# Attention and two mixtures of experts in one kernel: three branch programs for each expert of the second mixture, three up tiles of the next expert issued between the join and the next branch, and attention pieces in another order

## The chip, the cores and the metric

The kernel runs on one core of one Trainium2 chip. The metric is the device time of one execution in microseconds (us); the time shown is the median of 3 runs. The trace is one further execution, taken by the hardware profiler. The engines are named as in the trace: PE is the matrix engine (PEld its weight loads, PEq or PEldq its sequencers), DVE the vector engine, ACT the scalar engine, POOL GpSimd, SP the engine that issues most of the transfers.

## The reference, cut to what matters

Three stages stand one behind the other.

```python
# 1. chunked linear recurrence: 4 batches x 8 heads x 768 steps, head 32, state 16
M = (Cc @ Bc.T) * exp(cum_i - cum_j) * causal
y = M @ xc + (Cc @ state) * exp(cum)
state = exp(sum(la)) * state + (Bc * exp(cum_last - cum)).T @ xc
# 2. dense mixture: 3072 tokens of width 256, 4 experts, hidden width 1024
out += p[:, e:e+1] * (relu(x @ w1[e]) @ w2[e])
# 3. routed mixture: 8 experts, one per token, at most 768 tokens each
expert = argmax(x @ w_gate); gate = softmax(x @ w_gate)[expert]
out[i] = gate[i] * (relu(x[i] @ w1[expert]) @ w2[expert])
```

With the inputs used here the eight experts of stage 3 get 836, 313, 184, 362, 215, 164, 196 and 802 tokens; what is over 768 is dropped.

## The kernel before

All matmuls of the mixtures are done as three products of a high and a low part (`w1h`, `w1l`, `xh`, `xl` and so on), so each tile of 128 hidden units needs six matmuls for the up product (two halves of the width 256, three products) and three per block of 128 tokens for the down product.

**Stages 1 and 2 are interleaved.** The dense mixture walks over seven batches of 128-token steps (BLOCKS: 2, 3, 4, 4, 4, 4, 3 steps). For each batch it runs four experts of eight hidden tiles; after each tile it calls `tick(b)`, a slot, so that there are two slots for each tile. A slot issues what a table has put at this slot (`at_slot`: weight splits, loads), then some of the side pieces: the attention of the following batch's steps, one group after the other, spread evenly over the slots by the formula in `tick`, which begins at slot `wait` (11 for batch 0, else 0). One attention step is the list of groups in `USUAL`: pack B and C into high and low parts (`high`, `low`; the low parts are written by DVE at L198, those of C into the one buffer `cbd`), a running product over the step (`prefix`, a scan by DVE, L206), the decay matrices (`decay`, scans by DVE, L174), the scores on PE (L221, which read `bp` and `cbd`), masks (L239), products (L251), the split of the result, and the next step's loads. Every engine works off its own instructions in the order in which the program issues them. The scheduler adds the semaphores.

**Stage 3 walks over the experts.** For each expert e from 1 on, all engines read its token count (`values_load`, on PE a TENSOR_LOAD at L1028) and branch at L1032: over 256 tokens the wide program (`first_block` with 384 token columns, then `second_block`, which branches at L757: over 384 tokens a second block of 384 is done), else the narrow program (256 columns). Both end in a join, from which the next expert's count and branch follow. Expert 0 is done outside of this with 384 columns and its own second block. So with these counts the path is: e0 with a second block, e1 wide without one, e2 narrow, e3 wide without one, e4, e5 and e6 narrow, e7 wide with a second block. `ahead_of(e + 1)` marks the place of an instruction by which PE's sequencer is told in advance that a branch of the next expert lies ahead and where it likely goes; it is the first thing in each block.

`expert_block` runs the eight up tiles (L719 to L721, the relu to `gh` on ACT at L724, the low part `gl` on DVE at L725) and, behind them by LAG = 2 tiles, the down products (L736 to L738). `extra` are the next expert's row loads, transposes (`turn`, L689) and weight splits, issued between tiles.

Of the kernel before, what the change touches and what calls it, by code (L numbers as in the profile page):

```python
# [29 lines left out]
BIG = 1 << 20  # L30
SLOTS = 384
NARROW = 256
BLOCKS = [2, 3, 4, 4, 4, 4, 3]
MOST = max(BLOCKS)
NMAX = MOST * P
# [30 lines left out]
def attention_moe_moe_kernel(ctx: ExitStack, tc: tile.TileContext, aps: dict, cap: int):  # L66
# [88 lines left out]
    def attention_pieces(s, xH, xL, col):  # L155
# [151 lines left out]
            split=[split_high, split_low], state=[state_up], keep=[keep])  # L307

    USUAL = [g.split() for g in (
        "high0", "low0 high1", "", "low1 high2", "", "prefix0 low2 load2 load1", "", "decay0", "scores0", "mask0",  # L310
        "decay1 load0", "scores1 state_in0", "", "mask1", "", "products0", "split0", "split1 state0")]
    FIRST = [g.split() for g in (
        "prefix0 load2", "decay0", "", "scores0 decay1", "load0 load1", "state_in0", "mask0", "mask1", "", "products0", "split0",
# [383 lines left out]
            nc.scalar.copy(xh[:, d], t[d])  # L697
            nc.vector.tensor_tensor(xl[:, d], t[d], xh[:, d].bitcast(F32), ALU.subtract)

    def expert_block(e, k, n, extra):  # L700
        w1h, w1l, w2h, w2l = W[2, e]
        xh, xl = xs[e, k]
        g = gi[e, k]
        hs = {}
        y = []
        at_ = 0

        def go():
            nonlocal at_
            at_ += 1  # L710
            for p in extra.get(at_, []):
                p()

        for f in range(NF + LAG):
            if f < NF:
                ph = ps.tile([P, n], F32, tag="ph", name=f"qh{e}_{k}_{f}")
                for d in range(KD):
                    c = slice(FF * d + P * f, FF * d + P * f + P)
                    nc.tensor.matmul(ph, lhsT=w1h[:, c], rhs=xh[:, d, :n], start=d == 0, stop=False)  # L719
                    nc.tensor.matmul(ph, lhsT=w1h[:, c], rhs=xl[:, d, :n], start=False, stop=False)  # L720
                    nc.tensor.matmul(ph, lhsT=w1l[:, c], rhs=xh[:, d, :n], start=False, stop=d == KD - 1)  # L721
                hh = hp_.tile([P, n], F32R, tag="hh", name=f"gh{e}_{k}_{f}")
                hl = hp_.tile([P, n], F32R, tag="hl", name=f"gl{e}_{k}_{f}")
                nc.scalar.activation(hh, ph, AF.Relu)  # L724
                nc.vector.scalar_tensor_tensor(hl, ph, 0.0, hh.bitcast(F32), ALU.max, ALU.subtract)  # L725
                hs[f] = (hh, hl)
                go()
            js = [f - LAG] if LAG <= f < NF else list(range(NF - LAG, NF)) if f == NF else []
            for st in range(n // P):
                if js and js[0] == 0:  # L730
                    y.append(ps.tile([P, DM], F32, tag="acc", name=f"yy{e}_{k}_{st}", bufs=3))
                q = slice(P * st, P * st + P)
                for j in js:
                    hh, hl = hs[j]
                    c = slice(DM * j, DM * j + DM)
                    nc.tensor.matmul(y[st], lhsT=hh[:, q], rhs=w2h[:, c], start=j == 0, stop=False)  # L736
                    nc.tensor.matmul(y[st], lhsT=hh[:, q], rhs=w2l[:, c], start=False, stop=False)  # L737
                    nc.tensor.matmul(y[st], lhsT=hl[:, q], rhs=w2h[:, c], start=False, stop=j == NF - 1)  # L738
            if js:
                go()  # L740
        for st in range(n // P):
            o = gp.tile([P, ROW], F32, tag="row", name=f"yo{e}_{k}_{st}", bufs=MOST)[:, :DM]
            nc.scalar.activation(o, y[st], AF.Copy, scale=g[:, st, 0:1])  # L743
            i = nc.gpsimd.indirect_dma_start(  # L744
                out=out[:, :],
                out_offset=bass.IndirectOffsetOnAxis(ap=g.bitcast(I32)[:, st, 1:2], axis=0),
                in_=o[:, :], in_offset=None, bounds_check=TOK - 1, oob_is_err=False)
            disjoint("out", i)
# [4 lines left out]
            tc.mark_branch_hint_location(f"wide{e}", "LikelyTaken", engines=[mybir.EngineType.PE])  # L753

    def second_block(e, tokens):
        if nblk > 1:
            with tc.If(tokens > SLOTS, label=f"more{e}"):  # L757
                ahead_of(e + 1)
                expert_block(e, 1, SLOTS, {})
                for k in range(2, nblk):  # L760
                    with tc.If(tokens > SLOTS * k):
                        load_rows(e, k)
                        turn(e, k)
                        turned(e, k)
                        expert_block(e, k, SLOTS, {})


    new_xT(0)
# [119 lines left out]
    for b, i, e, c in (  # L888
# [23 lines left out]
    def tick(b):  # L912
        nonlocal slot, done
        nslot = 2 * sum(v[0] == b for v in seq)
        for fn in wq.get((b, slot), []):
            fn()
        if b == 1 and fills and slot % 3 == 2:
            fills.pop(0)()
        if b == 1 and slot == nslot - 1:
            while fills:  # L920
                fills.pop(0)()
        if urgent:
            urgent.pop(0)()
        wait = 11 if b == 0 else 0
        while done < len(side) and done < math.ceil((slot + 1 - wait) * len(side) / (nslot - 6 - wait)):
            side[done]()
            done += 1
        slot += 1
# [58 lines left out]
    for e, k in ahead:  # L987
        place(e, k)

    def first_block(e, n):  # L990
        extra = {}

        def add(i, fn):
            extra.setdefault(i, []).append(fn)

        add(0, lambda: ahead_of(e + 1))
        if n == SLOTS and nblk > 1:
            add(1, lambda: load_rows(e, 1))
            add(6, lambda: turn(e, 1))
            add(8, lambda: turned(e, 1))  # L1000
        if e + 1 < E2:
            add(1, lambda: load_rows(e + 1, 0))
            add(10, lambda: turn(e + 1, 0))
            add(12, lambda: turned(e + 1, 0))
        for c in range(4 if e + 2 < E2 else 0):
            m, i = (4, 6, 8, 10)[c], 4 * (e + 2) + c
            add(m, lambda w=order[i], lo=(nc.vector if c in (1, 2) else nc.gpsimd): split_w(2, *w, lo))
            if i + 5 < len(order):
                add(m + 3, lambda w=order[i + 5]: load_w(2, *w))
        for fn in extra.pop(0):  # L1010
            fn()
        expert_block(e, 0, n, extra)

    known = nc.values_load(cnt[0][0:1, 0:1], min_val=0, max_val=TOK)
    with tc.If(known > SLOTS - 1) as full:
# [2 lines left out]
    with full.Else():  # L1018
# [5 lines left out]
        turn(0, 0)  # L1024
        turned(0, 0)
        expert_block(0, 0, SLOTS, {4: [finish_ahead]})
    for e in range(E2):
        tokens = nc.values_load(cnt[1][0:1, e:e + 1], min_val=0, max_val=TOK)  # L1028
        if e == 0:
            second_block(e, tokens)  # L1030
            continue
        with tc.If(tokens > NARROW, label=f"wide{e}") as wide:  # L1032
            first_block(e, SLOTS)
            second_block(e, tokens)
        with wide.Else():
            first_block(e, NARROW)


def prepare(inputs):
# [51 lines left out]
```

## Time and profile before

| | |
|---|---|
| median of 3 runs | 809.57 us (809.2 to 809.78) |
| profiled execution | 811.7 us |
| its span in the trace | 809.9 us |
| PE busy | 774.8 us (96%) |
| DVE busy | 435.3 us (54%) |
| ACT busy | 283.4 us (35%) |
| POOL busy | 198.0 us (24%) |

The profiled execution is 2.1 us longer than the median of the runs, and 1.8 us of its time lie outside of the span that the trace shows. Busy shares are means over stages: stages 1 and 2 run to about 620 us, stage 3 behind them to about 805 us.

### The profile page before, as it was taken

To read this page: it belongs to the slowest core of one execution; us is meant where nothing else is said; L and a number is where in the kernel's file an instruction comes from. 1 tells how busy PE (TensorE), PEld (TensorE's weight loads), DVE (VectorE), ACT (ScalarE), POOL (GpSimd) and SP (SyncE) were. 2 spreads that over 40 slices of the span, in tenths; PEclk is the share of its full clock that TensorE was granted. 3 is DMA by queue.
4 is the path that set the end of the run, shared out by engine and by line. 5 is a ranking of instruction groups with operands and counts; after the bars stand their busy time and mean duration, and the time that the engine had idled before them with its cause. 6 is when DMAs were issued, how large, how long until landed. Compare 5 with 4: busy or idle time off the path is not lost. (4 is left out here: it accounts for less than half of the span.)

```text
span 809.9 us, 12519 instructions
## 1 busy us (share of the span) xinstructions
PE 774.8 (96%) x4752; PEld 688.7 (85%) x4752; DVE 435.3 (54%) x839; ACT 283.4 (35%) x550; POOL 198.0 (24%) x223
## 2 busy tenths in 40 slices
PE   9999989999999999999999999999999996968997
PEld 7889988977888778878788888889999896968997
DVE  5786777566664566655656546542534323524431
ACT  1443433323333232233322332322454333536432
POOL 1010202222110131211212202111665322525321
PEclk9999999999999999999999999999999998979999
DMA  8662677522210232202322013040353304544100
GB/s 256 219 188 78 209 206 212 171 82 102 81 61 18 82 108 82 82 0 82 105 82 82 28 55 108 14 140 11 114 159 104 115 21 143 158 141 131 32 23 28
DMA packets 50987, 83.26 MB, mean 103 GB/s; under 512 B 5136, under 2 KB 35809, under 8 KB 50908
## 3 DMA queue, kind: packets, MB, share of 16 engines
q1 hardware_dynamic: 47140, 75.30, 29.5%
q0 software_dynamic: 2400, 6.11, 2.1%
q10 hardware_dynamic: 1368, 0.81, 0.5%
q8 instruction: 49, 0.80, 0.4%
q14 instruction: 30, 0.25, 0.1%
HBM read 66.36 MB, written 16.31 MB: 102 GB/s over the span
## 5 line engine op out<-in xcount | busy, mean ns | idle before, releaser
L496 DVE SCALAR_TENSOR_TENSOR hl<-ph,hh 128x512 fp32r<-128x512 f32 (+2 forms) x216 | 133.5, 618 | 230.6 <-ACT hh L495 223.8
L495 ACT ACTIVATE hh<-ph 128x512 fp32r<-128x512 f32 (+2 forms) x216 | 117.2, 543 | 349.6 <-PE ph L492 342.0
L490 PE MATMUL ph<-xh,w1h 128*128 128x512 f32 (+2 forms) x432 | 160.4, 371 | 1.2 <-DVE hl L496 1.2
L519 PE MATMUL acc<-hh,w2h 128*128 128x512 f32 (+2 forms) x432 | 158.4, 367 | 1.1 <-DVE x L535 1.0
L491 PE MATMUL ph<-xl,w1h 128*128 128x512 f32 (+2 forms) x432 | 156.5, 362 | 0.0
L492 PE MATMUL ph<-xh,w1l 128*128 128x512 f32 (+2 forms) x432 | 156.3, 362 | 0.0
L520 PE MATMUL acc<-hl,w2h 128*128 128x512 f32 (+2 forms) x432 | 156.3, 362 | 0.0
L521 PE MATMUL acc<-hh,w2l 128*128 128x512 f32 (+2 forms) x432 | 156.1, 361 | 0.0
L725 DVE SCALAR_TENSOR_TENSOR gl<-qh,gh 128x384 fp32r<-128x384 f32 (+1 forms) x80 | 40.2, 503 | 106.0 <-ACT gh L724 97.6
L519 PEld LDWEIGHTS acc<-hh,w2h 128*128 128x128 f32 x432 | 81.2, 188 | 13.7 <-issue 2.0
L543 POOL TENSOR_TENSOR x<-x,cmb 128x512 f32<-128x512 f32 (+2 forms) x40 | 49.0, 1245 | 176.8 <-DVE cmb L540 176.8
L490 PEld LDWEIGHTS ph<-xh,w1h 128*128 128x128 f32 x432 | 81.3, 188 | 12.2 <-issue 1.7
L492 PEld LDWEIGHTS ph<-xh,w1l 128*128 128x128 f32 x432 | 81.2, 188 | 10.5
L521 PEld LDWEIGHTS acc<-hh,w2l 128*128 128x128 f32 x432 | 81.3, 188 | 10.4
L520 PEld LDWEIGHTS acc<-hl,w2h 128*128 128x128 f32 x432 | 81.3, 188 | 9.3
L491 PEld LDWEIGHTS ph<-xl,w1h 128*128 128x128 f32 x432 | 81.3, 188 | 8.7
L724 ACT ACTIVATE gh<-qh 128x384 fp32r<-128x384 f32 (+1 forms) x80 | 35.9, 448 | 92.5 <-PE qh L721 87.2
L174 DVE TENSOR_TENSOR_SCAN lt<-abc,id 128x512 f32<-128x512 f32 x44 | 59.6, 1354 | 0.1
L738 PE MATMUL yy<-w2h,gl 128*128 128x256 f32 x208 | 59.1, 284 | 0.0
L737 PE MATMUL yy<-w2l,gh 128*128 128x256 f32 x208 | 59.1, 284 | 0.0
L736 PE MATMUL yy<-w2h,gh 128*128 128x256 f32 x208 | 59.1, 284 | 0.0
L719 PE MATMUL qh<-sxh,w1h 128*128 128x384 f32 (+1 forms) x128 | 43.5, 340 | 16.3 <-issue 14.8
(156 smaller groups left out, 1075.2 us busy)
## 6 DMA issues: line engine op xcount, KB each, us to landing
stg<-in_w SPq DMA_DIRECT2D x34, 512.0 KB, 4.2
abc<-a_zero SPq DMA_DIRECT2D x21, 512.0 KB, 5.6
bcr<-in_bc SPq DMA_DIRECT2D x19, 512.0 KB, 3.9
disp<-zrow SPq DMA_DIRECT2D x12, 516.0 KB, 6.1
nat<-in_nat SPq DMA_DIRECT2D x24, 256.0 KB, 6.5
rw<-disp SPq DMA_DIRECT2D x12, 387.0 KB, 4.3
pb<-pT SPq DMA_DIRECT2D x16, 256.0 KB, 4.1
out<-zrow SPq DMA_DIRECT2D x6, 512.0 KB, 4.8
```

Source lines behind the costliest of these rows:

```text
L174: nc.vector.tensor_tensor_scan(t["lt"][:, sl, :].rearrange("p h i -> p (h i)"), a_bc[:, sl, :].rearrange("p h i -> p (h i)"), id4.rearrang ...
L490: nc.tensor.matmul(ph[:, :n], lhsT=wh[:, c], rhs=xh[:, k, :n], start=k == 0, stop=False)
L491: nc.tensor.matmul(ph[:, :n], lhsT=wh[:, c], rhs=xl[:, k, :n], start=False, stop=False)
L492: nc.tensor.matmul(ph[:, :n], lhsT=wl[:, c], rhs=xh[:, k, :n], start=False, stop=k == KD - 1)
L495: nc.scalar.activation(hh[:, :n], ph[:, :n], AF.Relu)
L496: nc.vector.scalar_tensor_tensor(hl[:, :n], ph[:, :n], 0.0, hh[:, :n].bitcast(F32), ALU.max, ALU.subtract)
L519: nc.tensor.matmul(a[:, :n], lhsT=wh[:, c], rhs=hh[:, :n], start=f == 0, stop=False)
L520: nc.tensor.matmul(a[:, :n], lhsT=wh[:, c], rhs=hl[:, :n], start=False, stop=False)
L521: nc.tensor.matmul(a[:, :n], lhsT=wl[:, c], rhs=hh[:, :n], start=False, stop=f == NF - 1)
L736: nc.tensor.matmul(y[st], lhsT=hh[:, q], rhs=w2h[:, c], start=j == 0, stop=False)
L737: nc.tensor.matmul(y[st], lhsT=hh[:, q], rhs=w2l[:, c], start=False, stop=False)
L738: nc.tensor.matmul(y[st], lhsT=hl[:, q], rhs=w2h[:, c], start=False, stop=j == NF - 1)
```

## The change

In words:

- **Three programs.** For e of 1 to 7 the branch on the second block is moved to the front: the wide program is chosen first (L1056), and inside it the choice between "384 and a second block" and "384 alone" (L1058). Three whole programs stand in the code for each expert, and `first_block` no longer tests for a second block in its middle. The row load and transposes for the second block are issued in that one program alone. `preferred_fallthrough_block` says which of the two programs stands right behind the branch.
- **A head behind each join.** `head(e + 1)` runs for every path between the join of expert e and the branch of expert e + 1: it marks the hint again and issues the first three up tiles (HEAD = 3) of the next expert for its first 256 columns. The block that follows only adds columns 256 to 383 of these tiles where it is wide (128-column matmuls), and begins at the fourth tile where it is narrow.
- **A fixed ring.** The tiles `hh` and `hl` come from three fixed pairs instead of the pool, since the head's tiles are read by other blocks. Six one-column memsets on POOL set them up.
- **Attention.** `USUAL` has `low1 high2` and `low2` two groups sooner, ahead of `prefix0`; `decay0` one group sooner; the loads in two groups. `wait` is 4 instead of 0 for batches 1 and on. Four weight splits of batch 1 go to the slots 7, 19, 31, 42 instead of 8, 16, 24, 32.

```diff
+HEAD = 3
     USUAL = [g.split() for g in (
-        "high0", "low0 high1", "", "low1 high2", "", "prefix0 low2 load2 load1", "", "decay0", "scores0", "mask0",
+        "high0", "low0 high1", "low1 high2", "low2 load1", "prefix0 load2", "", "decay0", "", "scores0", "mask0",
...
+    def make_ring():
+        for i in range(3):
+            ring.append([hp_.tile([P, NMAX], F32R, tag=t, name=f"ring_{t}{i}") for t in ("hh", "hl")])
+            for v in ring[-1]:
+                nc.gpsimd.memset(v.bitcast(F32)[:, 0:1], 0.0)
+    def up_part(e, k, f, a, b):
+        w1h, w1l = W[2, e][:2]
         xh, xl = xs[e, k]
+        ph = ps.tile([P, b - a], F32, tag="ph", name=f"qh{e}_{k}_{f}")
+        for d in range(KD):
+            c = slice(FF * d + P * f, FF * d + P * f + P)
+            nc.tensor.matmul(ph, lhsT=w1h[:, c], rhs=xh[:, d, a:b], start=d == 0, stop=False)
...
+        hh, hl = [v[:, a:b] for v in ring[f % len(ring)]]
+        nc.scalar.activation(hh, ph, AF.Relu)
+        nc.vector.scalar_tensor_tensor(hl, ph, 0.0, hh.bitcast(F32), ALU.max, ALU.subtract)
+    def head(e):
+        if e < E2:
+            ahead_of(e)
+            for f in range(HEAD):
+                up_part(e, 0, f, 0, NARROW)
+    def expert_block(e, k, n, extra, have=0):
...
             if f < NF:
-                ph = ps.tile([P, n], F32, tag="ph", name=f"qh{e}_{k}_{f}")
...
+                a = NARROW if f < have else 0
+                if a < n:
+                    up_part(e, k, f, a, n)
                 go()
...
-            (1, 8, 0, 2), (1, 16, 0, 3), (1, 24, 0, 0), (1, 32, 0, 1)):
+            (1, 7, 0, 2), (1, 19, 0, 3), (1, 31, 0, 0), (1, 42, 0, 1)):
...
-        wait = 11 if b == 0 else 0
+        wait = 11 if b == 0 else 4
...
+    make_ring()
...
-        if n == SLOTS and nblk > 1:
+        if two:
             add(1, lambda: load_rows(e, 1))
...
-        expert_block(e, 0, n, extra)
+        expert_block(e, 0, n, extra, HEAD)
...
-        with tc.If(tokens > NARROW, label=f"wide{e}") as wide:
-            first_block(e, SLOTS)
-            second_block(e, tokens)
-        with wide.Else():
-            first_block(e, NARROW)
+            with tc.If(tokens > NARROW, label=f"wide{e}", preferred_fallthrough_block=True) as wide:
+                if nblk > 1:
+                    with tc.If(tokens > SLOTS, preferred_fallthrough_block=False) as more:
+                        first_block(e, SLOTS, two=True)
+                        second_block(e, tokens)
+                    with more.Else():
+                        first_block(e, SLOTS)
...
+            with wide.Else():
+                first_block(e, NARROW)
+        head(e + 1)
```

The two places that matter most are shown by the instructions on an engine. The first is PE at the join of expert 1 and the branch of expert 2, before: the last down product of e1 (`yy_0_1`), the jump to the join, the count, the branch, and the first tile (`qh_0_0`) of the first program in the code.

```order
L738 MATMUL yy_0_1_7338<-w2h_1_5754,gl_0_7_7442 128x256
L1032 UNCONDITIONAL_BRANCH
L1028 TENSOR_LOAD cnt_97
L1032 COMPARE_AND_BRANCH
L1087 BRANCH_PREFETCH_HINT
L719 MATMUL qh_0_0_7490<-sxh_5732,w1h_2_5934 128x384
```

After, the branch stands behind the head: the rows below are the last six of its 18 matmuls of 256 columns (tiles `qh_0_0`, `qh_0_1`, `qh_0_2`), then the count, the two branches and the first 128-column matmul of the wide program.

```order
L717 MATMUL qh_0_2_7599<-sxh_5732,w1h_2_5934 128x256
L718 MATMUL qh_0_2_7599<-sxl_5733,w1h_2_5934 128x256
L719 MATMUL qh_0_2_7599<-sxh_5732,w1l_2_5935 128x256
L717 MATMUL qh_0_2_7599<-sxh_5732,w1h_2_5934 128x256
L718 MATMUL qh_0_2_7599<-sxl_5733,w1h_2_5934 128x256
L719 MATMUL qh_0_2_7599<-sxh_5732,w1l_2_5935 128x256
L1050 TENSOR_LOAD cnt_97
L1056 COMPARE_AND_BRANCH
L1058 COMPARE_AND_BRANCH
L1118 BRANCH_PREFETCH_HINT
L717 MATMUL qh_0_0_7991<-sxh_5732,w1h_2_5934 128x128
```

What moved: between the jump out of the last block and the branch now stand a hint and 18 matmuls that do not depend on the count; the wide program behind the branch begins with six 128-column matmuls per tile for three tiles.

The second is DVE in the attention step whose scores PE runs at 265 us. `cbd` is the low part of C, `pre` the prefix scan, `lt` a decay scan, `hl` the low part of a relu and `cmb` a combine of the dense mixture. Before:

```order
L198 SCALAR_TENSOR_TENSOR cbd<-bcr_2566,cst,cbd 64x4x128
L540 TENSOR_TENSOR cmb_0_0_2791<-acc_0_0_2636,pb_0_2455 128x512
L540 TENSOR_TENSOR cmb_0_1_2793<-acc_0_1_2637,pb_0_2455 128x512
L496 SCALAR_TENSOR_TENSOR hl_1_2_2805<-ph_1_2_2797,hh_1_2_2804 128x512
L206 SCALAR_TENSOR_TENSOR pre_2808<-an_2564,zero_88 128x128
L198 SCALAR_TENSOR_TENSOR cbd<-bcr_2566,cst,cbd 64x4x128
L174 SCALAR_TENSOR_TENSOR lt_2827<-abc_2618,id_87 128x512
```

After, in the same step (`lg` and `bp` belong to the routing and to the low part of B):

```order
L199 SCALAR_TENSOR_TENSOR bp_2802<-bcr_2558,cst,bp_2802 128x512
L199 SCALAR_TENSOR_TENSOR cbd<-bcr_2558,cst,cbd 64x4x128
L497 SCALAR_TENSOR_TENSOR hl_1_3_2826<-ph_1_3_2818,hh_1_3_2825 128x512
L199 SCALAR_TENSOR_TENSOR cbd<-bcr_2558,cst,cbd 64x4x128
L207 SCALAR_TENSOR_TENSOR pre_2844<-an_2568,zero_88 128x128
L497 SCALAR_TENSOR_TENSOR hl_1_4_2858<-ph_1_4_2850,hh_1_4_2857 128x512
L571 COPY lg_2840<-rows_0_2841 128x8
L175 SCALAR_TENSOR_TENSOR lt_2866<-abc_2629,id_87 128x512
```

What moved: both `cbd` rows now stand ahead of `pre`, and one `hl` and the routing's copy stand between `pre` and `lt`; before, the second `cbd` stood between `pre` and `lt`.

## Rows read from the trace of the kernel before

**Rows 1.** The page: its span, and granted clock by 40 slices (tenths).

```profile
span 809.9 us, 12519 instructions
...
PEclk9999999999999999999999999999999998979999
```

**Rows 2.** Waits of PE, whole span: us in total, times, longest.

```profile
PE qh L719 <- issue: 14.8, 3, 6.4
PE sc L221 <- DVE cbd L198: 5.9, 7, 1.4
...
PE y L251 <- DVE m L239: 1.2, 2, 1.1
```

**Rows 3.** Timeline of PE near 265 us: start, us, what [idle before].

```profile
265.17 0.48 PE L221 MATMUL sc<-cbd,bp 128*128 128x256 f32 x2 [1.00 <-DVE cbd L198]
```

**Rows 4.** Timeline of DVE, 260 to 265 us, columns as in Rows 3.

```profile
260.00 0.73 DVE L198 SCALAR_TENSOR_TENSOR cbd<-bcr,cst,cbd 64x512 fp32r<-64x512 f32 x1
...
262.72 1.51 DVE L206 TENSOR_TENSOR_SCAN pre<-an,zero 128x128 f32<-128x128 f32 x1
264.27 0.75 DVE L198 SCALAR_TENSOR_TENSOR cbd<-bcr,cst,cbd 64x512 fp32r<-64x512 f32 x1
265.05 1.36 DVE L174 TENSOR_TENSOR_SCAN lt<-abc,id 128x512 f32<-128x512 f32 x1
```

**Rows 5.** Timeline of PE around two joins (e1 to e2, e4 to e5).

```profile
678.45 0.28 PE L738 MATMUL yy<-w2h,gl 128*128 128x256 f32 x1
684.95 0.55 PE L719 MATMUL qh<-sxh,w1h 128*128 128x256 f32 x1 [6.22 <-issue]
...
739.64 0.28 PE L738 MATMUL yy<-w2h,gl 128*128 128x256 f32 x1
742.12 0.36 PE L719 MATMUL qh<-sxh,w1h 128*128 128x256 f32 x1 [2.20 <-issue]
...
744.21 0.39 PE L719 MATMUL qh<-sxh,w1h 128*128 128x256 f32 x1 [0.43 <-DVE gl L725]
```

**Rows 6.** Line 757 on PE's sequencer, 676 to 681 us: ns min/median/max, first start.

```profile
L757 PEldq COMPARE_BRANCH  x2: 351/1212/2072, 676.7 to 678.9; - x2
L757 PEldq EVENT_SEMAPHORE  x1: 51/51/51, 678.8 to 678.8; - x1
```

**Rows 7.** Line 1032 on PE's sequencer, four windows with one branch each.

```profile
L1032 PEldq COMPARE_BRANCH  x1: 3197/3197/3197, 681.5 to 681.5; - x1
...
L1032 PEldq COMPARE_BRANCH  x1: 79/79/79, 698.8 to 698.8; - x1
...
L1032 PEldq COMPARE_BRANCH  x1: 2742/2742/2742, 739.1 to 739.1; - x1
...
L1032 PEldq COMPARE_BRANCH  x1: 331/331/331, 754.4 to 754.4; - x1
```

**Rows 8.** DMA queues from 681.5 to 684.7 us: packets, MB, share.

```profile
q8 instruction: 1, 0.02, 1.8%
```

**Rows 9.** After the two long gaps: busy us by engine, clock, DMA.

```profile
684.90:691.30 6.40, 6.35 (x34) 6.23 (x35) 1.27 (x3) 2.31 (x5) 0.44 (x1) 0.62 0.01 3
724.70:731.50 6.80, 6.75 (x33) 6.63 (x34) 1.27 (x3) 2.19 (x5) 0.84 (x1) 0.55 0.01 2
```

**Rows 10.** Timeline of PE: pace at 384, 256 and 128 columns.

```profile
660.01 0.34 PE L720 MATMUL qh<-sxl,w1h 128*128 128x384 f32 x1
660.18 0.34 PE L721 MATMUL qh<-sxh,w1l 128*128 128x384 f32 x1
...
742.43 0.28 PE L721 MATMUL qh<-sxh,w1l 128*128 128x256 f32 x1
742.55 0.28 PE L719 MATMUL qh<-sxh,w1h 128*128 128x256 f32 x1
...
734.80 0.82 PE L689 MATMUL tr<-cst,rw 128*128 128x128 f32 x6
735.37 0.36 PE L719 MATMUL qh<-sxh,w1h 128*128 128x256 f32 x1
```

More of the change, by code (lines that the diff above doesn't have):

```diff
@@ L698, in turned @@
             nc.vector.tensor_tensor(xl[:, d], t[d], xh[:, d].bitcast(F32), ALU.subtract)
-    def expert_block(e, k, n, extra):
-        w1h, w1l, w2h, w2l = W[2, e]
-        xh, xl = xs[e, k]
+    ring = []
+    def make_ring():
[5 more added lines that the diff above has]
+        w1h, w1l = W[2, e][:2]
+        xh, xl = xs[e, k]
+        ph = ps.tile([P, b - a], F32, tag="ph", name=f"qh{e}_{k}_{f}")
+        for d in range(KD):
+            c = slice(FF * d + P * f, FF * d + P * f + P)
+            nc.tensor.matmul(ph, lhsT=w1h[:, c], rhs=xh[:, d, a:b], start=d == 0, stop=False)
+            nc.tensor.matmul(ph, lhsT=w1h[:, c], rhs=xl[:, d, a:b], start=False, stop=False)
+            nc.tensor.matmul(ph, lhsT=w1l[:, c], rhs=xh[:, d, a:b], start=False, stop=d == KD - 1)
+        hh, hl = [v[:, a:b] for v in ring[f % len(ring)]]
[7 more added lines that the diff above has]
+    def expert_block(e, k, n, extra, have=0):
+        w2h, w2l = W[2, e][2:]
         g = gi[e, k]
-        hs = {}
         y = []
@@ L715, in expert_block @@
             if f < NF:
-                ph = ps.tile([P, n], F32, tag="ph", name=f"qh{e}_{k}_{f}")
[L717 to L726, printed above, removed]
+                a = NARROW if f < have else 0
+                if a < n:
+                    up_part(e, k, f, a, n)
                 go()
@@ L733, in expert_block @@
                 for j in js:
-                    hh, hl = hs[j]
+                    hh, hl = ring[j % len(ring)]
                     c = slice(DM * j, DM * j + DM)
@@ L755, in second_block @@
     def second_block(e, tokens):
[L756 to L765, printed above, removed]
+        ahead_of(e + 1)
+        expert_block(e, 1, SLOTS, {})
+        for k in range(2, nblk):
+            with tc.If(tokens > SLOTS * k):
+                load_rows(e, k)
+                turn(e, k)
+                turned(e, k)
+                expert_block(e, k, SLOTS, {})
     new_xT(0)
@@ L988, in attention_moe_moe_kernel, with first_block @@
         place(e, k)
-    def first_block(e, n):
+    make_ring()
+    def first_block(e, n, two=False):
         extra = {}
@@ L1029, in attention_moe_moe_kernel @@
         if e == 0:
-            second_block(e, tokens)
-            continue
-        with tc.If(tokens > NARROW, label=f"wide{e}") as wide:
-            first_block(e, SLOTS)
-            second_block(e, tokens)
-        with wide.Else():
-            first_block(e, NARROW)
+            if nblk > 1:
+                with tc.If(tokens > SLOTS):
+                    second_block(e, tokens)
+        else:
+            with tc.If(tokens > NARROW, label=f"wide{e}", preferred_fallthrough_block=True) as wide:
+                if nblk > 1:
+                    with tc.If(tokens > SLOTS, preferred_fallthrough_block=False) as more:
+                        first_block(e, SLOTS, two=True)
+                        second_block(e, tokens)
+                    with more.Else():
+                        first_block(e, SLOTS)
+                else:
+                    first_block(e, SLOTS)
+            with wide.Else():
+                first_block(e, NARROW)
+        head(e + 1)
 def prepare(inputs):
```

## The prediction

> **What bounds the kernel now.** I read the page first: a span of 809.9 us and a row of granted clock that is full but for two dips behind nine tenths of the span [rows 1]. PE is busy nearly all the time, so only three things can shorten the kernel: waits of PE, a lower clock, and fewer or shorter matmuls. The list of PE's waits puts them in order [rows 2]: 14.8 us in three waits of the kind "issue", in which PE waits for nothing that the trace shows as a semaphore; then 5.9 us in seven waits of the scores (L221) for `cbd` from DVE; the rest is about 1 us each. The rows of single waits then say where they lie.
>
> *The joins.* The last matmul of expert 1 begins at 678.45 and the first of expert 2 comes after a gap of 6.22 us; from e4 to e5 the gap is 2.20 us [rows 5]. The third, from e3 to e4, is the longest of the row at 6.4. PE's sequencer shows what fills the long one. It comes to the second block's branch (L757) at 676.7, about 1.8 us ahead of PE; it then stands before a semaphore until 678.8, when PE has ended; the jump to the join takes 2.07 us [rows 6]; the branch at L1032 takes another 3.197 [rows 7]. During that branch exactly one transfer of 0.02 MB runs on the queue of instructions [rows 8]: the code of the target is fetched. The same branch costs 0.079 us where the next program in memory is taken, 2.742 from e4 to e5, and 0.331 from e5 to e6 [rows 7]; I read the last as a target that the hint had fetched in time.
>
> *The clock.* Behind the two long gaps PE runs at a granted clock of 0.62 for 6.40 us and 0.55 for 6.80 us [rows 9], partly at the lower level of 1.2 GHz; nowhere else is there a dip after the start [rows 1].
>
> *The attention.* At 265.17 PE waited 1.00 us for `cbd` [rows 3]. DVE wrote one part of it at 260.00, then ran the scan `pre` for 1.51 us from 262.72, and only then, at 264.27, the second part [rows 4]. The other longest waits have the same order.
>
> **The change part by part.** All is summed as a difference, on the profiled execution's 811.7 us (809.9 of span and 1.8 around it), and carried to the median of the runs, 809.57.
>
> *Attention pieces.* Both `cbd` writes now stand ahead of `pre`. The scan's 1.51 us and the order that put it ahead are what the 1.00 us at 265.17 is made of; with 0.75 us of `cbd` alone [rows 4] the scores are free before PE comes to them. Of the 5.9 us I take 4.9 as gained. The 1.0 left is for one wait that comes up elsewhere: `decay0` (1.36 us, [rows 4]) now runs sooner, and what follows it on DVE, a `hl` that PE's down products need, is late by as much once; the products' wait for the mask, 1.2 us in two [rows 2], stays. Bounds: 0 (all waits move) and −5.9. The later start of the side pieces and the four moved splits change when DVE is busy, not how much it does; I put them at nothing, since DVE is idle for nearly half of the span, and their risk is in the bound of 0. The memsets of the ring are six one-column operations on POOL; the row copies behind them on POOL are read only when stage 3 begins. I put them at nothing too.
>
> *Branches and fetched code.* Before: 14.8 [rows 2] and 0.20 more behind the 0.331 branch [rows 7], 15.0 in all. After, the wide program without a second block has no branch in its middle, so the sequencer's wait for PE's end at L757 [rows 6] is gone and the jump to the join begins with its lead of 1.8. A jump to code that isn't there costs about 2.7 [rows 7], so 0.9 shows, at the joins behind e1 and e3: 1.8. Next the head: a hint, then 18 matmuls. At 0.12 each ([rows 10]: 742.43 to 742.55) they give 2.15 us, the third tile waits 0.43 for a free buffer [rows 5], and loading the count takes about 0.3 (at most the 0.5 between the end of the jump, 678.9 + 2.07, and the branch's start at 681.5, [rows 6, 7]): 2.9 us from hint to branch. The fetch needs 2.7 to 3.2 [rows 7]. So it is there, or nearly, and the branch costs its 0.331, with 0.3 for the load and 0.3 for the first weights. That is 0.9 behind each of e1 and e3 (1.8) and 0.6 at each of the two joins from narrow to narrow (1.2). A wide program stands right behind its branch and costs 0.079. Finally, code is longer now, and by my own count of PE's instructions there are three more places at which a block begins just ahead of a piece of code that isn't there yet: the entry from e0, the narrow program of e6, and e7's second branch, which is taken. No row shows these; each lies between 0 (fetched in time) and 3.2 (the longest of [rows 7]). I take 5.8 of 9.6, since [rows 7] has two full fetches, one hit and one near-full among its branches that leave the line. After: 1.8 + 1.8 + 1.2 + 5.8 = 10.6, a gain of 4.4. Bounds: 10.2 (no such places) and 0.6 (all three in full).
>
> The Trainium skill's page "Runtime: NRT & Kernel Launch", section "Instruction fetch mechanics", says that crossing from one 16 KiB piece of code to the next is mostly hidden, since fetching runs ahead in sequence. By that rule the three places would cost nothing and the sum would be 796.7. The branches of [rows 7] that leave the line don't bear on it; no row here shows a plain crossing that costs.
>
> *The clock.* Half-rate stretches cost (1 − 0.62) × 6.40 + (1 − 0.55) × 6.80 = 5.5 us [rows 9]. Two waits of 0.43 at the third tile were hidden behind the slow matmuls and come back, so 4.6. The gaps at these joins shrink from over 6 to about 1.8, the sum of the jump's 0.9 and the branch's 0.9, with 2 us of work between them; the gap of 2.20 from e4 to e5 [rows 5] left the clock full [rows 1]. But the places of unknown cost could bring a new dip, so I keep half: −2.3. Bounds: −4.6 and 0.
>
> *Split tiles in a wide program.* The first three tiles of e1, e3 and e7 run as 256 and 128 columns. A 384-column matmul takes 0.17, a 256-column one 0.12 and a 128-column one 0.095 (six transposes in 0.57), all [rows 10]: 18 × (0.12 + 0.095 − 0.17) = 0.8. To this come 0.25 for the wait for a buffer that shorter tiles bring (0.43 at worst, [rows 5]), 0.3 for the count and branches without a lead, and 0.15 for three more relus of short tiles: +1.5 each, +4.5 in all. Bounds +1.1 (128 columns at 0.07, a third of 384 rounded up, and no waits) and +6.3 (0.12, as 256 columns).
>
> *Sum.* −4.9 − 4.4 − 2.3 + 4.5 = −7.1: 804.6 on the profiled execution, **802.5** on the median. All lower ends together give 790, all upper ends 815.
>
> **The rivals.** *A: the hint comes too late, slower.* If each narrow target is fetched only when its branch is resolved, or the fetch begins late, four narrow entries cost 3.3 each (3.197 and the load), two jumps to the join 0.9, and e7's taken branch 2.9 (between 2.742 and 3.197, [rows 7]): 17.9 against 15.0. The clock's dips stay, split tiles cost 4.5 and the attention gives 4.9: 809.57 + 2.9 + 4.5 − 4.9 = **812.1**. It decides at the 2.9 us between hint and branch against the fetch's 2.7 to 3.2. For it speaks the 2.742 from e4 to e5, which had a hint too, a whole block ahead; against it the 0.331 from e5 to e6 [rows 7]. The same page and section of the Trainium skill has a rule that gives this: a taken branch to code outside of the two pieces held forces a fetch before execution goes on. The 3.197 with its one transfer agrees, the 0.331 does not.
>
> *B: the attention's waits only move.* DVE does the same work between the same matmuls, and a `hl` or mask comes late instead: 802.5 + 4.9 = **807.4**. For it: the scans are as long as before. Against it: DVE has idle time, and the waits for `hl` and masks are now about 1 us each in all [rows 2].
>
> *C: the new places cost nothing and the clock stays up.* −4.9 − 10.2 − 4.6 + 4.5: **794.4**. For it: crossing ahead in sequence cost nothing that I could find before; against: the entry from e0 comes when the sequencer has no lead.
>
> *D: the wide program isn't behind its branch.* Then three wide entries pay 2.9 each: **811.2**. The order of the branches in the code speaks against it.
>
> **How the numbers follow.** Main case 0.60, A 0.13, B 0.10, C 0.12, D 0.05. The runs before lie within 0.6 us of one another, so I take 0.2% (1.6 us) as what a measurement can tell from no change. The main case with its own bounds runs from 797.5 to 807.5, nearly all of it faster; with C and most of B that is 0.75 faster. B's and A's edges give 0.11 for the same; A, D and the main case's upper tail give 0.14 for slower. The range is 796.5 to 811.5: it leaves out about half of C, and the upper halves of A and D, 0.18.
>
> **What would show it.** No waits of the scores for `cbd`, and none over 1 us for `hl` or masks in their place; "issue" waits behind e1 and e3 in two parts of about 0.9 with the head's 18 matmuls between; the branch at L1056 at about 0.3 for narrow and 0.08 for wide; a row of clock without the two dips; 128-column matmuls at a pace near 0.095. Wrong would be: the branch at 2.7 or more for narrow (A), new waits early in e1, e6 and e7 far from 5.8 in sum (C or its opposite), new waits in the attention (B), or 128 columns at the price of 256.

## The result, and the profile after

The changed kernel takes **802.69 us** (median of 4 runs, 801.27 to 802.99) against 809.38 (808.72 to 809.78) in the same job. The record gives the ratio of the runs as 0.9899, with a 95% interval of 0.9879 to 0.9919, so 6.6 to 9.8 us less; the two medians alone stand 6.7 apart, near the smaller end. The forecast was 802.5. The profiled execution took 801.27 with a span of 799.5, 10.4 us less than the one of before; 2.1 of these are the opening, which moves by up to 3.6 us from trace to trace (below), so two spans must not simply be subtracted.

The page of the changed kernel, span and granted clock:

```profile
span 799.5 us, 12626 instructions
...
PEclk9999999999999999999999999999999999999999
```

At this grain the two dips of [rows 1] are gone. The list of PE's waits of the changed kernel (us in total, times, longest):

```profile
PE qh L717 <- issue: 6.0, 5, 2.8
PE qh L718 <- issue: 2.7, 1, 2.7
PE yy L757 <- ACT ring_hh L721: 1.7, 2, 1.0
...
PE y L252 <- DVE m L240: 0.5, 2, 0.3
...
PE sc L222 <- DVE cbd L199: 0.2, 1, 0.2
```

The scores' wait for `cbd` fell from 5.9 to 0.2, and the 14.8 of "issue" of [rows 2] became 6.0 + 2.7. The 1.7 us put down to `ring_hh` belong to them as well: the product that waits reads the head's first tile, whose relu was over long before (730.75 for the product at 733.23), and what ends there is a branch (below). In the step of [rows 3, 4], DVE and then PE now read, in the timeline:

```profile
259.52 0.75 DVE L199 SCALAR_TENSOR_TENSOR cbd<-bcr,cst,cbd 64x512 fp32r<-64x512 f32 x1
260.30 0.42 DVE L207 TENSOR_TENSOR_SCAN pre<-an,zero 128x128 f32<-128x128 f32 x1
```

```profile
264.39 0.40 PE L222 MATMUL sc<-cbd,bp 128*128 128x256 f32 x2
```

`cbd` is finished at 260.27, ahead of `pre`, and PE comes to the scores at 264.39 without a wait. The scan `pre` itself takes 0.42 us here, not the 1.51 of [rows 4]. The timeline of PE at e1's first tiles:

```profile
653.82 0.28 PE L718 MATMUL qh<-sxl,w1h 128*128 128x128 f32 x1
653.93 0.28 PE L719 MATMUL qh<-sxh,w1l 128*128 128x128 f32 x1
...
654.69 0.33 PE L717 MATMUL qh<-sxh,w1h 128*128 128x128 f32 x1 [0.16 <-issue]
657.68 0.47 PE L718 MATMUL qh<-sxl,w1h 128*128 128x128 f32 x1 [2.66 <-issue]
```

The reader sees two things. Two 128-column matmuls stand 0.11 us apart, no nearer than 256 columns in [rows 10]. And in the middle of the third split tile, with no branch near it, PE stops for 2.66 us, from 655.02 on; in this wait one transfer runs on the queue of instructions q8, from 655.46 to 656.42. At the joins e1 to e2 and e4 to e5:

```profile
675.87 0.28 PE L759 MATMUL yy<-w2h,ring_hl 128*128 128x256 f32 x1
678.95 0.38 PE L717 MATMUL qh<-sxh,w1h 128*128 128x256 f32 x1 [2.80 <-issue]
...
682.69 0.55 PE L757 MATMUL yy<-w2h,ring_hh 128*128 128x256 f32 x1 [0.20 <-issue]
...
733.23 0.36 PE L757 MATMUL yy<-w2h,ring_hh 128*128 128x256 f32 x1 [0.99 <-ACT ring_hh L721]
```

The gap of 6.22 us in [rows 5] is now one of 2.80 ahead of the head and one of 0.20 behind it; that of 2.20 is one of 0.99. The sequencer's branches, the jumps out of e1 and e3 at L1058 first, then the branches into e2, e3, e5 and e6 at L1056 (compare [rows 6, 7]):

```profile
L1058 PEldq COMPARE_BRANCH  x1: 4643/4643/4643, 674.1 to 674.1; - x1
...
L1058 PEldq COMPARE_BRANCH  x1: 4343/4343/4343, 711.3 to 711.3; - x1
...
L1056 PEldq COMPARE_BRANCH  x1: 1164/1164/1164, 681.3 to 681.3; - x1
...
L1056 PEldq COMPARE_BRANCH  x1: 69/69/69, 695.7 to 695.7; - x1
...
L1056 PEldq COMPARE_BRANCH  x1: 1195/1195/1195, 731.8 to 731.8; - x1
...
L1056 PEldq COMPARE_BRANCH  x1: 331/331/331, 745.7 to 745.7; - x1
```

The jump out of e1 begins at 674.1, 1.7 us ahead of PE's last matmul (675.87), and lasts 4.64 us. In the first part of it, up to 675.9, the queue q8 moves nothing; from 675.9 to 678.8 it moves one transfer:

```profile
q8 instruction: 1, 0.02, 2.5%
```

The stretches with a low clock (busy us by engine, granted clock, DMA), to be held against [rows 9]:

```profile
657.60:663.00 5.40, 5.32 (x23) 5.32 (x24) 0.58 (x2) 1.49 (x3) 1.32 (x1) 0.50 0.01 3
680.10:683.50 3.40, 3.20 (x15) 2.72 (x14) 1.27 (x3) 1.13 (x4) 0.00 (x0) 0.50 0.03 6
```

Both are at 0.50, the lower of the two levels. They follow the gaps of 2.66 and 2.80; behind the jump out of e3 (2.50) there is none. In the second trace of the same kernel (changed_again) it is the other way round: the second stretch follows the jump out of e3 (2.46) and none follows e1's (2.67).

**Where the time went.** Spans hide what each stage does, so the table reads the traces between fixed places. The opening is read up to the 145th matmul of the dense mixture's up products, stages 1 and 2 from there to the last down product of that mixture, and stage 3 from there to the last down product of all (starts in the timeline of PE, all in us):

| profiled execution | opening | stages 1, 2 | stage 3 |
|---|---|---|---|
| before | 58.27 | 562.02 | 183.52 |
| changed | 56.14 | 555.07 | 182.17 |
| changed_again | 56.27 | 555.16 | 181.61 |
| attention_alone | 55.67 | 555.11 | 183.31 |
| mixture_alone | 58.08 | 562.11 | 181.67 |
| table_alone | 55.73 | 557.55 | 184.03 |
| start_and_splits_alone | 57.87 | 556.66 | 182.15 |
| head_0 | 58.44 | 555.10 | 187.37 |
| no_hint_in_head | 57.77 | 555.06 | 184.14 |
| shift_20 | 54.88 | 555.10 | 180.97 |
| shift_40 | 57.66 | 555.08 | 180.21 |
| shift_96 | 56.19 | 555.08 | 195.41 |
| shift_200 | 57.77 | 555.16 | 190.69 |
| attention_shift_96 | 55.57 | 555.11 | 180.99 |

So the change is worth 6.95 us in stages 1 and 2 and 1.35 in stage 3 (1.91 in its second trace): 8.3, which lies in the interval. Stages 1 and 2 repeat within 0.1 us wherever the attention is the same. Stage 3 does not: it takes 182.15 to 184.03 in the four unpadded traces with the old joins and 181.61 to 182.17 in the three with the changed ones (changed, changed_again, mixture_alone), so one trace of each does not give its gain.

Added up over all of PE's instructions, stage 3 splits into idle time, what the low clock takes while PE works (half of the busy time at 0.50), and the rest, work at full clock. The old joins have 17.9 to 18.4 us idle and 159.5 to 160.0 of work, the new ones 13.0 to 13.8 idle and 164.0 to 164.1 of work: about 5 us of waiting are saved and about 4 are paid back in longer work. The clock's part makes the difference from trace to trace: 3.8 to 6.7 with the old joins, 4.3 to 4.6 with the new.

### The profile page after: what moved, and what is told of

It reads as the page before. It is cut to its first block, busy times and chain, and to the rows that moved or that the text cites. A ratio compares the mean times of both kernels' runs of the same rounds, so it can differ in the third digit from the quotient of the medians.

```text
span 799.5 us, 12626 instructions
## 1 busy us (share of the span) xinstructions
PE 774.0 (97%) x4794; PEld 689.2 (86%) x4794; DVE 429.7 (54%) x844; ACT 283.8 (35%) x555; POOL 187.4 (23%) x227
## 4 chain that ended last, share of the span: by engine, by line
PE 92%; DVE 3%; issue 2%; ACT 1%; DMA 0%; POOLq 0%; POOL 0%; ACTq 0%; DVEq 0%
PE ph L491 11%; PE acc L520 11%; PE ph L492 10%; PE ph L493 10%; PE acc L521 10%; PE acc L522 10%; PE qh L717 3%; PE yy L757 3%; PE yy L759 3%; PE yy L758 3%; PE qh L718 3%; PE qh L719 3%; PE y L252 2%; PE sc L222 1%; PE y L248 1%
## 5 line engine op out<-in xcount | busy, mean ns | idle before, releaser
L722 DVE SCALAR_TENSOR_TENSOR ring_hl<-qh,ring_hh 128x256 fp32r<-128x256 f32 (+2 forms) x89 | 41.7, 469 | 106.0 <-ACT ring_hh L721 97.4
L520 PEld LDWEIGHTS acc<-hh,w2h 128*128 128x128 f32 x432 | 81.3, 188 | 13.8 <-DVE x L536 1.6
L522 PEld LDWEIGHTS acc<-hh,w2l 128*128 128x128 f32 x432 | 81.3, 188 | 10.4
L721 ACT ACTIVATE ring_hh<-qh 128x256 fp32r<-128x256 f32 (+2 forms) x89 | 37.4, 420 | 89.6 <-PE qh L719 79.3
L757 PE MATMUL yy<-w2h,ring_hh 128*128 128x256 f32 x208 | 59.9, 288 | 2.1 <-ACT ring_hh L721 1.7
L759 PE MATMUL yy<-w2h,ring_hl 128*128 128x256 f32 x208 | 59.3, 285 | 0.0
L758 PE MATMUL yy<-w2l,ring_hh 128*128 128x256 f32 x208 | 59.3, 285 | 0.0
L175 DVE TENSOR_TENSOR_SCAN lt<-abc,id 128x512 f32<-128x512 f32 x44 | 57.5, 1306 | 0.0
L717 PE MATMUL qh<-sxh,w1h 128*128 128x256 f32 (+2 forms) x146 | 46.7, 320 | 7.2 <-issue 6.0
```

The source lines that it names most:

```text
L520: nc.tensor.matmul(a[:, :n], lhsT=wh[:, c], rhs=hh[:, :n], start=f == 0, stop=False)
L522: nc.tensor.matmul(a[:, :n], lhsT=wl[:, c], rhs=hh[:, :n], start=False, stop=f == NF - 1)
L717: nc.tensor.matmul(ph, lhsT=w1h[:, c], rhs=xh[:, d, a:b], start=d == 0, stop=False)
```

## The experiments

Theory: the attention's order carries the gain, since what the joins save is paid again in code that isn't there, split tiles and clock. Rival: the three programs and their head carry it.

**attention_alone**: the kernel before with the attention's edits only.

```diff
-        "high0", "low0 high1", "", "low1 high2", "", "prefix0 low2 load2 load1", "", "decay0", "scores0", "mask0",
+        "high0", "low0 high1", "low1 high2", "low2 load1", "prefix0 load2", "", "decay0", "", "scores0", "mask0",
...
-            (1, 8, 0, 2), (1, 16, 0, 3), (1, 24, 0, 0), (1, 32, 0, 1)):
+            (1, 7, 0, 2), (1, 19, 0, 3), (1, 31, 0, 0), (1, 42, 0, 1)):
...
-        wait = 11 if b == 0 else 0
+        wait = 11 if b == 0 else 4
```

> The kernel before with the attention pieces in the new order only (table of groups, start of the side pieces, four weight splits). First theory: it carries most of the gain, as the two traces say: from the first up tile behind the opening to the last product of the dense mixture the changed kernel is 6.9 us shorter, of which 5.7 are waits of the scores for cbd; expected 802.5 us against 809.4. Rival (the size that the prediction gave it): 4.9 us, 804.5. If the gain is the second mixture's, it stays within 1.6 us of 809.4.

Measured: 803.05 us (801.98 to 804.8) against 811.74 in the same job, ratio 0.9898 (0.9884 to 0.9912). Its waits of PE:

```profile
PE qh L719 <- issue: 15.1, 3, 6.4
...
PE sc L221 <- DVE cbd L198: 0.2, 1, 0.2
```

By the runs this is the whole gain, with the old joins untouched; by the stages it is 7.1 of the 8.3.

**mixture_alone**: the changed kernel with the three edits above undone.

> The changed kernel with the attention pieces in the old order: three programs, head and ring only. First theory: what was saved at the joins is nearly all paid again by a wait for code in the middle of e1, a second stretch at the half clock and split tiles: 1.4 us less than before, 808.0. Rival (the prediction's own terms): 2.2 less, 807.2. If the head is worth the whole difference of the joins, 5 us or more, 804 or less.

Measured: 808.78 (807.03 to 810.45), ratio 0.9960 (0.9948 to 0.9972), 1.9 us less in stage 3. Its waits:

```profile
PE sc L222 <- DVE cbd L199: 5.9, 7, 1.4
PE qh L717 <- issue: 5.5, 2, 2.8
PE qh L718 <- issue: 2.9, 1, 2.9
```

The three programs are worth 2.3 to 4.2 us by the runs and 1.8 by the stages, and the order of the parts is as the theory had it. The two ratios together would make 0.986, a little more than the whole change (0.9899, upper gain 0.9879); by the stages 7.1 + 1.8 stand against 8.3.

**table_alone**: the first of the three attention edits. **start_and_splits_alone**: the other two.

> The kernel before with the new table of groups (USUAL) alone; the side pieces begin at slot 0 and the four weight splits stay as before. First theory: the table is what takes the waits for cbd away; what the later start and the moved splits add is the products' wait for the mask behind a split, 1.08 us once, as in the trace of before: 5.8 to 6.9 us less than before. Rival: new waits come up in the places that the later start was to clear, and the table alone gives under 4 us.

> The kernel before with the later start of the side pieces (wait 4) and the four moved weight splits alone, the old table of groups. First theory: the two parts of the attention change add up, so this gives what the table alone left, 4.1 us (the first two stages 601.3 instead of 605.4). Rival: it does something only together with the table, and alone it gives under 1 us.

Measured: table 806.07, ratio 0.9946 (0.9928 to 0.9964), stages 1 and 2 shorter by 4.5; start and splits 805.55, ratio 0.9948 (0.9929 to 0.9966), shorter by 5.4. Waits of PE from 20 to 621 us, the table alone first:

```profile
PE acc L519 <- DVE x L535: 2.1, 2, 1.0
PE y L251 <- DVE m L239: 1.3, 2, 1.1
...
PE acc L519 <- DVE cmb L540: 1.2, 2, 0.9
```

```profile
PE sc L221 <- DVE cbd L198: 1.0, 2, 0.7
...
PE y L251 <- DVE m L239: 0.5, 2, 0.3
```

The table fell short of what was expected, the other two did more, and they don't add up. The table does take all waits for `cbd` away, but leaves 1.3 on the mask and adds about 1 each on `x` and `cmb`. The later start and the moved splits take 4.9 of the 5.9 away with the old table, and 0.7 of the 1.2 on the mask. Together the two give 6.95, not 9.8: they remove largely the same waits. Which of the start and the splits does it was not run.

How the start and the splits can do it with `cbd` still behind `pre` shows in the length of that scan: all of them before and in start_and_splits_alone (ns min/median/max, first to last start), then POOL's work of before near 262 us:

```profile
L206 DVE TENSOR_TENSOR_SCAN pre<-an,zero x20: 406/414/1514, 10.7 to 521.7; 128x128 f32<-128x128 f32 x20
...
L206 DVE TENSOR_TENSOR_SCAN pre<-an,zero x20: 406/415/425, 10.9 to 516.0; 128x128 f32<-128x128 f32 x20
...
261.42 2.54 POOL L543 TENSOR_TENSOR x<-x,cmb 128x512 f32<-128x512 f32 x2 [19.43 <-DVE cmb L540]
```

The scan of [rows 4] runs from 262.72 to 264.24 beside this addition on POOL, which ends at 263.96. Before, 4 of the 20 scans take 0.91 to 1.51 us; all four run beside an addition into `x` and end 0.28 to 0.29 behind its end. Three of them stand ahead of waits for `cbd`, which make 2.6 of the 5.9 us. The five long ones of table_alone (0.80 to 1.14) do the same; there `cbd` is out of the way. In start_and_splits_alone and in the changed kernel no scan meets an addition, and all take 0.41 to 0.43. One at 83.22 before met the last 0.10 us of an addition and took 0.41. Why a scan is held there was not tested.

**head_0**: the changed kernel with no up tiles in the head. **no_hint_in_head**: without the hint there.

```diff
-HEAD = 3
+HEAD = 0
```

```diff
         if e < E2:
-            ahead_of(e)
             for f in range(HEAD):
```

> The changed kernel without the head's up tiles: the hint stands right ahead of the count and the branch, and no tile is split. First theory: the tiles hide the fetch of the narrow programs; without them e2, e4, e5 and e6 wait about 2.9 each (11.6 against 2.1), the wide programs save 3.5 on split tiles, and the clock falls behind the long gaps as before: 5 to 7 us more than the changed kernel. Rival: what the head hides it pays back in split tiles and clock, so the time stays within 2 us of the changed kernel.

> The changed kernel without the hint behind the join; the one at the start of each first block stays. First theory: the fetch seen right behind that hint (at 679.45, 716.37 and 730.51 of the changed kernel's trace) is what makes the branch to narrow cheap; without it these branches cost 2.7 or more, some 5 us in all over the changed kernel. Rival: the hint of the block before is enough, no change.

Measured: head_0 809.2, ratio 0.9979 (0.9965 to 0.9992), stage 3 longer than the changed kernel's by 5.2, as the first theory had it. The joins e1 to e2, e3 to e4 and e4 to e5 in its timeline:

```profile
677.71 0.57 PE L717 MATMUL qh<-sxh,w1h 128*128 128x256 f32 x1 [6.05 <-issue]
...
716.78 0.57 PE L717 MATMUL qh<-sxh,w1h 128*128 128x256 f32 x1 [5.95 <-issue]
...
734.86 0.57 PE L717 MATMUL qh<-sxh,w1h 128*128 128x256 f32 x1 [3.86 <-issue]
```

So 6 us again behind e1 and e3 instead of about 3, and 3.86 instead of 0.99: the branches into e2, e4 and e5 take 2.5 to 4.4 us with nothing ahead of them, which the up tiles cover, and without them three programs are slower than the old two. e7's second branch costs 2.85 here against 0.12. Its code also lies elsewhere than the changed kernel's, and place alone moves such waits (below), so the 5.2 is not the tiles' alone. Without the hint: 803.78, ratio 0.9911 (0.9889 to 0.9933), not to be told from the changed kernel; the join e1 to e2 and the branches into e2 and e5:

```profile
680.35 0.39 PE L717 MATMUL qh<-sxh,w1h 128*128 128x256 f32 x1 [2.86 <-issue]
...
L1055 PEldq COMPARE_BRANCH  x1: 839/839/839, 682.7 to 682.7; - x1
...
L1055 PEldq COMPARE_BRANCH  x1: 756/756/756, 735.8 to 735.8; - x1
```

Here the first theory fell: the branches into e2, e4, e5 and e6 take 0.84, 1.17, 0.76 and 0.33 us without that hint, against 1.16, 1.04, 1.20 and 0.33 with it (1.01, 0.45, 0.81 and 0.33 in changed_again). Stage 3 is 2.0 longer in this trace, but its idle time is not (13.2 against 13.8); the low clock takes 7.6 instead of 4.3. Whether the hint at the start of the block before is needed was not run.

**shift_20, shift_40, shift_96, shift_200**: the changed kernel with 10, 20, 48 and 100 matmuls (two instructions of PE each) in the program for e0 that these counts never run. All that is executed is the same (12626 instructions in each trace); its code lies later.

```diff
         expert_block(0, 0, SLOTS, {4: [finish_ahead]})
+        pad = ps.tile([P, P], F32, tag="s", name="pad", bufs=3)
+        for _ in range(20):
+            nc.tensor.matmul(pad, lhsT=u_b, rhs=ones_b, start=True, stop=True)
```

> The changed kernel with 20 matmuls (40 instructions of PE) added at the end of the program for e0 that never runs with these counts, so all code behind it lies 40 instructions later and nothing else that is executed differs. First theory: the wait of 2.66 us in e1's third split tile is code that isn't there yet, since a transfer's end falls 16 instructions into e1; moved by 40 the branch comes behind that end and the wait is gone, and with it the half clock behind it (2.7 us): 797.5 against 802.7. Rival: the wait belongs to the split tiles or their buffers; it stays, and the time with it, 802.7.

> As the last one, with 96 instructions. First theory: the end of a transfer now falls 14 instructions into e3, not e1, so a wait of 2.7 us moves from e1's third split tile to e3's, with a half clock behind it or not: 800 to 803. Rival: e1 keeps its wait and e3 has none, 802.7.

> The changed kernel with 20 instructions of PE that never run ahead of e0's second block. First theory: 20 is enough to bring e1's branch behind the end of its transfer (the wait in e1's third tile goes, with the half clock behind it) and little enough to leave e0's second block clear of it, which 40 did not (a new wait of 1.83): 796 to 799. Rival: the waits only move from place to place and their sum stays: 801 to 804.

> The changed kernel with 200 instructions of PE that never run ahead of e0's second block; by my count no head and no branch of the executed path then lies across the end of a transfer, only e5's narrow program begins 12 instructions ahead of one. First theory: e1's wait and the half clock behind it go, no new wait of over 2 us comes up, the two jumps of 2.5 to 2.8 stay: third stage 177, time 797 to 799. Rival: a wait comes up elsewhere as with 20 and 40, third stage 180 or more.

Measured: shift_20 802.04 (798.93 to 804.12), ratio 0.9898 (0.9878 to 0.9918); shift_40 806.27 (800.94 to 809.21), 0.9936 (0.9919 to 0.9952); shift_96 813.85 (809.89 to 818.46), 1.0025 (1.0004 to 1.0045); shift_200 811.7 (809.0 to 814.72), 1.0014 (0.9997 to 1.0032). Rows of PE's timeline, shift_20 (its profiled execution, 798.93, is its fastest):

```profile
653.42 0.33 PE L717 MATMUL qh<-sxh,w1h 128*128 128x128 f32 x1 [0.16 <-issue]
...
742.10 0.36 PE L757 MATMUL yy<-w2h,ring_hh 128*128 128x256 f32 x1 [3.46 <-issue]
```

shift_40 (its profiled execution, 800.94, is its fastest):

```profile
637.09 0.48 PE L718 MATMUL qh<-sl,w1h 128*128 128x384 f32 x1 [1.83 <-issue]
...
676.97 0.39 PE L717 MATMUL qh<-sxh,w1h 128*128 128x256 f32 x1 [0.22 <-DVE ring_hl L722]
...
681.14 0.28 PE L758 MATMUL yy<-w2l,ring_hh 128*128 128x256 f32 x1 [1.08 <-issue]
```

shift_96:

```profile
636.63 0.66 PE L717 MATMUL qh<-sh,w1h 128*128 128x384 f32 x1 [4.06 <-issue]
...
679.11 0.38 PE L717 MATMUL qh<-sxh,w1h 128*128 128x256 f32 x1 [2.64 <-issue]
...
682.46 0.58 PE L718 MATMUL qh<-sxl,w1h 128*128 128x256 f32 x1 [2.63 <-issue]
...
688.39 0.55 PE L757 MATMUL yy<-w2h,ring_hh 128*128 128x256 f32 x1 [2.55 <-ACT w1h L366]
```

shift_200:

```profile
638.33 0.66 PE L717 MATMUL qh<-sh,w1h 128*128 128x384 f32 x1 [4.10 <-issue]
...
722.95 0.55 PE L757 MATMUL yy<-w2h,ring_hh 128*128 128x256 f32 x1 [3.20 <-issue]
```

e1's wait of 2.66 is gone in all four: there is none behind 653.42 in shift_20, where the changed kernel had it behind 654.69. It stands in changed_again (2.61) and mixture_alone (2.93) too, which have the same stage 3. That the place of the code made it is shown, and by the transfer inside it, code not yet there. But others come up: 3.46 at e6, 1.83 in e0's second block and 1.08 in e2, 4.1 at the jump out of e0's first block, and with 96 a row of 2.64, 2.63 and 2.55 at one join. In e7, where the changed kernel loses 0.12, they are 1.52 with 40, 3.38 with 96 and 3.18 with 200. The rival of shift_20 ("only move from place to place") is nearer to the truth; my counts of where the waits would move (e3 with 96, none over 2 us with 200) were wrong. In shift_40 the jump out of e1 costs nothing: the first wait behind it is 0.22 for a buffer, at 676.97. The medians of the runs say that no padding tried is faster than none by more than the noise.

**attention_shift_96**: attention_alone with the same 48 matmuls. **changed_again**: the changed kernel as it is.

> The kernel before with the new attention order (attention_alone) and 96 instructions of PE that never run ahead of e0's second block. First theory: where the code lies decides what its branches cost in the old layout as well; the third stage moves from 183.3 by 2 us or more, either way. Rival: only the three programs with their head are sensitive; 183 to 184.

> The changed kernel once more, beside the three others of this call. First theory: the spread of single times comes from the opening, whose first up tile begins between 10.7 and 15.1 us in the traces so far whatever the kernel; the stretch of the two first stages stays at 598.5 us and the third at 182 within 1. Rival: the third stage itself varies by several us from run to run.

Measured: attention_shift_96 801.11 (799.57 to 802.2), ratio 0.9890 (0.9869 to 0.9912); changed_again 801.53 (800.86 to 802.88), 0.9896 (0.9874 to 0.9918). The old layout moves too: stage 3 is 2.3 us shorter than unshifted, since the join e1 to e2 halves and the one from e4 to e5 costs nothing, although the jump out of e0's first block now costs 3.87. The joins e1 to e2 and e3 to e4:

```profile
676.35 0.36 PE L719 MATMUL qh<-sxh,w1h 128*128 128x256 f32 x1 [2.93 <-issue]
...
715.65 0.55 PE L719 MATMUL qh<-sxh,w1h 128*128 128x256 f32 x1 [6.55 <-issue]
```

So the old two programs at another place are as fast as the three at theirs: 801.11 and 801.53 in one job. changed_again repeats the stages within 0.6 us, though its first up tile begins 2 us sooner; the stretch behind it up to the mark swallows that.

## Why the prediction was right, and where it was not

The time was met (802.5 against 802.69), partly by luck: errors cancel, and one sum holds for this place of the code alone.

- **Attention: the mechanism right, the term too small and its reason split wrongly.** The forecast was −4.9, the stage gives −6.95. Of that, PE's idle time is 5.8 (7.4 to 1.6, all gaps added up); the other 1.1 lies in PE's pace and is not assigned. Its own term "the later start of the side pieces and the four moved splits ... I put them at nothing" failed: alone they take 5.4. I priced where DVE's work stands in its own order, but not beside what the even spread puts it. The 1.51 us that I took for the scan's own is one held beside POOL's addition; elsewhere it takes 0.41 to 0.43, and the start and the splits alone bring it there. Of the allowance of 1.0 for a wait that comes up elsewhere, a new 0.5 on `cmb` came.
- **Branches and code: the sum right by luck, the parts not.** Forecast 10.6 after, and idle of 10.7 in the timeline: two jumps 2.80 + 2.50, e1's crossing 2.66, the narrow entries 0.20 + 0.75 + 0.99 + 0.17, three small ones of 0.27, 0.16 and 0.23. "0.9 shows" of each jump failed: the lead of 1.8 hides nothing, since the transfer begins only about when PE comes to its own last matmul. Against that, of three places at 5.8 only one cost much, 2.66 in e1, with 0.17 at e6 and 0.12 at e7; the padded kernels show other sums. The narrow entries idle 2.1 in all against 3.0 forecast, but only e6's branch took the forecast 0.3; the other three took 1.0 to 1.2. The "two full fetches, one hit and one near-full" behind the 5.8 are one more than [rows 7] show: the branch into e4, 2.907 in the same trace, seems to be among them.
- **Crossing ahead in sequence is not always free.** The Trainium skill's page "Runtime: NRT & Kernel Launch", section "Instruction fetch mechanics", calls it mostly hidden; e1's 2.66 us, gone when the code lies 20 instructions later, is a case that isn't. Its rule on taken branches agrees with the jumps of 2.50 and 2.80, each with its transfer. The branches to narrow at 0.331 do not speak against it, as the prediction had it: the rule is on targets that are not held, and into e6 q8 moves nothing from 738.5 to 746.8, so the target was there.
- **Clock: half of the forecast.** −1.1 instead of −2.3: the two stretches cost 0.50 × (5.4 + 3.4) = 4.4 against 5.5 before. One follows the crossing that the change brought. The gaps at the joins behind e1 and e3, 1.8 in the forecast, are 3.0 and 3.25 in two parts.
- **Split tiles: 18 × (0.12 + 0.115 − 0.17) = 1.2 each, 3.5 in all, not 4.5.** 128 columns go at 0.11 to 0.12, near the forecast's upper bound, but the waits that I had added to them are in the branches' sum above, and the waits for a tile's low part fell from 1.8 to 1.2.

These terms of stage 3 make −4.3 − 1.1 + 3.5 − 0.6 = −2.5; measured is −1.35. Added up over all of PE's instructions, idle time fell by 4.4 (18.2 to 13.8), the clock's part by 1.1, and the work at full clock rose by 4.2 (159.9 to 164.1). So the missing 1.1 is 0.5 of idle time that the terms leave out and 0.7 of work beyond the 3.5; which instructions it is is not assigned. Rival A did not happen, since the fetch was there for e6 and nearly for the others; B did not, since no wait over 0.5 us took the place of `cbd`.

What stays open: what the fetch takes next at each place. My reading (a hint or a branch in the next piece decides) explained e1's wait and failed on shift_96 and shift_200. The runs of one padded kernel differ too: of shift_40's six, the two shortest (800.94 and 804.24) had a mean granted clock of 0.993 and 0.992, the four of 805.87 to 809.21 one of 0.983 to 0.984. Over 805 us the difference of 0.009 comes to about 7 us (estimate), enough for the longer times; what lowered the clock in them is in no trace.

## What to carry to other kernels

Where one engine is nearly always busy, look at what its short waits stand behind on the other engine's queue, and move the producer ahead of long instructions that nobody waits for. Compare such an instruction with others of its kind first: where it takes 1.51 us here and 0.41 elsewhere, look at what runs beside it on the other engines. Pacing side work by a few slots did as much here as reordering it, so price both from the trace. Where branches lie on the path, the place of the code is worth as much as its form: measure a change of layout at two or three paddings before the gain is put down to the idea, and compare stages between fixed instructions, not spans.

## What was not expected of the hardware

- A jump's fetch came with the engine, not with the sequencer: begun at 674.15, its transfer came at 675.96, PE's last matmul at 675.87, and 2.80 us were lost. In all 16 such jumps out of e1 and e3 that took over 4 us in these traces, the sequencer was 1.7 us ahead and the transfer came between 0.1 us ahead of and 0.6 behind PE's last matmul. What holds it back was not tested.
- A scan on DVE of 0.41 us took up to 1.51 when it began during an addition on POOL; in all ten such cases of before and table_alone it ended 0.28 to 0.31 us behind the addition's end.
- Twenty instructions that never run moved e1's wait away, and 96 made stage 3 longer by 13.2 us (195.41 against 182.17).
- The first up tile behind the opening begins between 10.7 and 15.1 us in kernels whose opening is the same; behind it, stages 1 and 2 repeat within 0.1 us where the attention is the same.
- A 128-column matmul takes the time of a 256-column one, 0.11 to 0.12 us.
